# Opening of a two-block transformer kernel: who computes the scale sums, who norms the first x tiles, who makes the last two rests of h

## The chip, the core and the metric

The kernel runs on one core of a Trainium2 chip. A core has five engines that each work through their own list of instructions in order: TensorE (PE, matrix products; PEld is its weight load), VectorE (DVE), ScalarE (ACT), GpSimd (POOL) and SyncE (SP), which here issues the transfers (DMA). The engines wait for each other by semaphores. On-chip data lies in SBUF (128 partitions); matrix products are written to PSUM, in banks of 128 x 512 float32. The metric is the device time of one execution in microseconds (us); less is better.

## The reference, cut to what matters

```python
mod = (silu(c) @ w_mod).reshape(c.shape[0], 6, 1, -1)     # c: 1 x 1024, w_mod: 1024 x 6144
sa, ca, ga, sb, cb, gb = (mod[:, 0], ..., mod[:, 5])      # six rows of 1024
h = layernorm(x) * (1 + ca) + sa                          # x: 2048 tokens x 1024
x = x + ga * attention(h, wq, wk, wv, wo, beta)           # 32 heads, 4 segments of 512 tokens with a memory
h = layernorm(x) * (1 + cb) + sb
x = x + gb * token_mlp(h, w1, b1, w2, b2)                 # MLP across the 2048 tokens, width 3584
```

The change touches only how `sa` (the shift), `ca` (the scale) and the first 512 rows of `h` are computed. Each entry of `sa` and `ca` is a dot product of 1024 products, silu(c) against one column of `w_mod`.

## The kernel before, in words

Everything is float32. A product of two float32 matrices is made from three matmuls: each operand is cut into a high part `hi` (a cast, line 123 on ScalarE or 125 on another engine) and a rest `lo = x - hi` (line 126), and hi*hi, hi*lo and lo*hi are added up in PSUM. The helper is `split(dst, src, hi_eng, lo_eng)`.

The **opening** makes h for segment 0 (tokens 0 to 511) and the projections of head group 0 from it.

- Four tiles of x (128 tokens x 1024) are loaded and normed in place by `norm_x` (line 215): `ln_stats` (line 128) takes mean and variance on VectorE (lines 131 and 133) and the inverse root with ScalarE's Ln and Exp (134, 135) and a refinement on VectorE (137 to 139); then one VectorE operation of one column makes the bias (217) and ScalarE writes `x*rstd + bias` over 1024 columns (218).
- silu(c) lies in two forms: `sc`, a column per chunk, and `scb`, the whole row repeated on all 128 partitions.
- h is made in 8 chunks `ct` of 128 channels. For each chunk two pieces of `w_mod`, tiles `wm` of 128 x 1024 (512 KB), are loaded: part 0 for the shift and part 1 for the scale. The shift sums come from VectorE: one scalar_tensor_tensor multiplies `wm` by `scb` and adds up each row (line 283). The scale sums of chunks 0 to 3 (`ct < NSC`, NSC = 4) come from TensorE (line 291: eight products 128x128 by 128x1 into a PSUM column). Those of chunks 4 to 7 come from POOL and ScalarE: POOL multiplies by `scb` in two halves of 512 columns (line 287), ScalarE adds up the rows by a copy with an accumulator (line 288). Line 295 adds 1 (`saca`).
- `h_chunk` (line 220) transposes the four x tiles' 128 channels on TensorE into a PSUM bank (line 223), applies scale and shift on ScalarE (225), and splits the result: in segment 0 `hi` on ScalarE and `lo` on POOL for all eight chunks. In segment 1, `hi` is on VectorE and `lo` on VectorE for odd chunks and POOL for even.
- `first_chunk(ct)` adds the chunk's 12 matmuls into keys and values (line 196, `nps`) and 3 into queries (204, `qps`). Meanwhile the first weights are split (`wv`, `wq`: hi on ScalarE, lo on VectorE).

After the opening, segment 1 follows in the same way (`seg_load(1)`, whose x tiles 4 to 7 are loaded behind the last `wm`; `seg_chunks`, `project`): the copies of k, v and the value parts (lines 358, 359, 364, 365) and the splits of q and k into `sg` for segment 0 stand between. Then come 32 rounds of attention (4 heads each; scores, maxima, exponentials, values), the output projection, and the token MLP in two large products.

Each engine's list is ordered by a planner that simulates the program with its own costs when the kernel is built; a change in the opening thus can shift instructions of the later attention rounds against each other. The transfers of the opening have one order on SyncE's queue: x 0 to 3, then the `wm` pieces and the first weights, then x 4 to 7. Eleven `wm` buffers exist, so the twelfth piece waits for the reader of the first. The host lays out the scale part of `w_mod` per chunk in the form that its engine needs (transposed for TensorE below `NSC`, row-wise from `NSC` on).

Of the kernel before, what the change touches and what calls it, by code (L numbers as in the profile page):

```python
# [13 lines left out]
ALU = mybir.AluOpType  # L14
# [16 lines left out]
LEADP, LEADS, NSK = 8, 3, 8  # L31
XB = 4
EARLY = (2, 3)
NSC = 4
VL = 1
PHB = 2
P32B = 2
# [10 lines left out]
def attention_and_mlp(ctx, tc, x, wq, wkv, wo, beta, w1, b1, w2, b2, c, wm_a, wm_b, out):  # L48
    nc = tc.nc
    V, A, G, T, SY = nc.vector, nc.scalar, nc.gpsimd, nc.tensor, nc.sync  # L50
# [18 lines left out]
    scb, gaw = (a.tile([P, D], F32, name=n) for n in ("scb", "gaw"))  # L69
# [8 lines left out]
    def bank(tag, bufs, name):  # L78
        return psum.tile([P, 512], F32, tag=tag, bufs=bufs, name=name)
# [39 lines left out]
    def split(dst, src, hi_eng, lo_eng):  # L119

        hi, lo = dst[:, 0], dst[:, 1]
        if hi_eng is A:
            A.copy(hi, src)  # L123
        else:
            hi_eng.tensor_copy(hi, src)
        lo_eng.tensor_tensor(lo, src, hi.bitcast(F32), op=ALU.subtract)  # L126

    def ln_stats(pool, src, tag):
        st = const.tile([P, 2, 6], F32, tag="st", bufs=4, name="st")
        for i in range(2):  # L130
            V.bn_stats(st[:, i], src[:, 512 * i:512 * i + 512])
        mv = const.tile([P, 4], F32, tag="mv", bufs=4, name="mv")
        V.bn_aggr(mv[:, 0:2], st)
        A.activation(mv[:, 2:3], mv[:, 1:2], AF.Ln, bias=eps)
        A.activation(mv[:, 2:3], mv[:, 2:3], AF.Exp, scale=-0.5)
        v, r0, t = mv[:, 1:2], mv[:, 2:3], mv[:, 3:4]
        V.tensor_scalar(t, v, EPS, r0, op0=ALU.add, op1=ALU.mult)
        V.tensor_scalar(t, t, -0.5, r0, op0=ALU.mult, op1=ALU.mult)
        V.tensor_scalar(r0, t, 1.5, r0, op0=ALU.add, op1=ALU.mult)
        return mv  # L140
# [4 lines left out]
    def new_page(name):  # L145
        return page.tile([P, 2, 512], F32R, tag="page", bufs=16, name=name)
# [17 lines left out]
    def load_part(g, pr, kind, part, res):  # L164

        if pr == 0:
            split_part(g, kind, part, fetch_part(g, kind, part))
            return
        for i in range(2):
            w = aw.tile([P, 2, 512], F32R, tag="w", bufs=8, name=f"w{kind}{pr}_{g}_{part}_{i}")  # L170
            SY.dma_start(w.bitcast(F32), wsp[g, 2 * part + i if kind == "v" else 4 + i])
            res[kind, 2 * part + i] = w
# [37 lines left out]
    def load_x(pool, tt):  # L210
        t = pool.tile([P, D], F32, tag="x", bufs=XB, name=f"x{tt}")
        SY.dma_start(t, x[P * tt:P * tt + P])
        return t

    def norm_x(pool, t):
        mv = ln_stats(pool, t, "a")
        V.tensor_scalar(mv[:, 3:4], mv[:, 0:1], -1.0, mv[:, 2:3], op0=ALU.mult, op1=ALU.mult)
        A.activation(t, t, AF.Identity, scale=mv[:, 2:3], bias=mv[:, 3:4])

    def h_chunk(pool, xs, seg, ct):  # L220
        ps = bank(*(("s1", 2), ("s2", 2))[ct % 2] if seg else ("s2", 2), f"hps{seg}_{ct}")
        for i in range(4):
            T.transpose(ps[:, 128 * i:128 * i + 128], xs[i][:, P * ct:P * ct + P], ident)
        h32 = pool.tile([P, L], F32, tag="h32", bufs=HB, name=f"h32_{seg}_{ct}")
        A.activation(h32, ps, AF.Identity, scale=saca[:, ct, 1:2], bias=saca[:, ct, 0:1])
        pg = new_page(f"h{seg}_{ct}")
        split(pg, h32, V if seg else A, V if seg and ct % 2 else G)
        hpages[seg, ct] = pg

    def token_tile(tt):  # L230

        r = gaw
        norm_x(a, r)
        for half in range(2):
            ps = bank("s2", 2, f"hpl{tt}_{half}")
            for i in range(4):
                ct = 4 * half + i
                T.transpose(ps[:, 128 * i:128 * i + 128], r[:, P * ct:P * ct + P], ident)
            for i in range(4):
                ct = 4 * half + i  # L240
                A.activation(r[:, P * ct:P * ct + P], ps[:, 128 * i:128 * i + 128], AF.Identity,
                             scale=saca[:, ct, 1:2], bias=saca[:, ct, 0:1])
        hi = a.tile([P, D], F32, tag="raw", bufs=3, name=f"hix{tt}")
        A.copy(hi.bitcast(F32R), r)
        for c in (slice(0, 512), slice(512, 1024)):
            G.tensor_tensor(r[:, c].bitcast(F32R), r[:, c], hi[:, c], op=ALU.subtract)
        i = tt % 4
        for part, t in enumerate((hi, r)):
            SY.dma_start(hT1[tt // 4 - 2, :, :, part, P * i:P * i + P].rearrange("k p n -> p k n"),
                         t.rearrange("p (k n) -> p k n", k=NK))  # L250
# [4 lines left out]
    s1p = left.__enter__()  # L255
    xs = {0: [load_x(s1p, tt) for tt in range(4)]}
# [10 lines left out]
    def first_chunk(ct):  # L267
        h = hpages[0, ct]
        for half in range(2):
            kv_chunk(W[0, 0], h, half, ct, two_tiles(first[half]))  # L270
        q_chunk(W[0, 0], h, ct, first[2])

    with tc.high_priority():
        for t in xs[0]:
            norm_x(s1p, t)
    scale_ps = bank("ms", 1, "scale")
    scs = s1p.tile([P, NK], F32, name="scs")
    for ct in range(NK):
        for part in range(2):
            wm = s1p.tile([P, D], F32, tag="wm", bufs=11, name=f"wm{ct}_{part}")  # L280
            last_wm = SY.dma_start(wm, wm_a[part, ct])
            if part == 0:
                V.scalar_tensor_tensor(wm, wm, 1.0, scb, op0=ALU.mult, op1=ALU.mult, accum_out=saca[:, ct, 0:1])
            elif ct >= NSC:
                for i in range(2):
                    c = slice(512 * i, 512 * i + 512)
                    G.tensor_tensor(wm[:, c], wm[:, c], scb[:, c], op=ALU.mult)
                A.activation(wm, wm, AF.Copy, accum_out=scs[:, ct:ct + 1])
            else:
                for k in range(NK):  # L290
                    T.matmul(scale_ps[:, ct:ct + 1], wm[:, P * k:P * k + P], sc[:, k:k + 1], start=(k == 0),
                             stop=(k == NK - 1), skip_group_check=True)
        if ct < 3:
            load_part(0, 0, *(("v", 0), ("q", 0), ("v", 1))[ct], W[0, 0])
        V.tensor_scalar_add(saca[:, ct, 1:2], (scale_ps if ct < NSC else scs)[:, ct:ct + 1], 1.0)
        h_chunk(s1p, xs[0], 0, ct)
        if ct:
            first_chunk(ct - 1)
# [260 lines left out]
    def seg_load(seg):  # L559
        seg_x[seg] = [load_x(s2p, tt) for tt in range(4 * seg, 4 * seg + 4)]  # L560
        for t in seg_x[seg]:
            norm_x(s2p, t)

    def seg_chunks(seg, lo, hi):
        for ct in range(lo, hi):
            h_chunk(s2p, seg_x[seg], seg, ct)
# [63 lines left out]
    for n in range(-LEADS, 4 * NI + VL):  # L630
# [4 lines left out]
        if 0 <= m + 4 < 4 * NI:  # L635
            t = (m + 4) // 4
# [5 lines left out]
        if 59 <= m < 67:  # L642
            seg, ct = 2 + (m - 59) // 4, 2 * ((m - 59) % 4)
            reload_h(seg, ct)
            reload_h(seg, ct + 1)
        if 4 * NI - 5 <= m < 4 * NI + 3:
            i = m - 4 * NI + 5
# [282 lines left out]
    for u, (ph, g) in enumerate(units):  # L930
# [59 lines left out]
        t = tp.tile([P, 3, 512], F32, tag="tu", bufs=1, name=f"tu{g}")  # L990
# [66 lines left out]
```

## Time and profile before

| what | value |
|---|---|
| median of 3 runs | 2281.92 us (2280.88 to 2282.4) |
| the profiled execution's own time | 2281.25 us |
| its span, first to last instruction | 2279.5 us |
| granted TensorE clock, mean | 0.989 |
| TensorE busy (matmul) | 2214.7 us, 97% |
| VectorE busy | 1671.9 us, 73% |
| ScalarE busy | 1148.1 us, 50% |
| POOL busy | 735.6 us, 32% |

Times in the timeline are us from the start of the span. A timeline row gives start and duration, engine, line and operation, output and inputs, shape, and in brackets the idle time of the engine before it with what ended it; a row with x2 merges two instructions in succession. The table of windows gives how long each engine was busy in a stretch, and the granted clock as a share of full speed. The busy time of an instruction on VectorE or POOL includes time in which it has been issued but stands still.

### The profile page before, as it was taken

The page shows a single profiled execution, that of the slowest core. Times are in us where ns is not written, and L with a number is a line of the kernel's source. Part 1 is how long each engine was busy: PE and PEld are TensorE (multiplying, and loading weights), DVE is VectorE, ACT ScalarE, POOL GpSimd, SP SyncE. Part 2 cuts the span into 40 slices and gives each one's busy share as a digit, 9 for nine tenths or more (in the row PEclk, how much of TensorE's full clock was granted, in tenths as well). Part 3 has the DMA queues.
Part 4 walks back from the last instruction along what each step waited for, and adds up shares of the span by engine and source line. Part 5 has one row for each costly group of instructions (what it writes and reads, how often), then busy time and mean ns, then how long its engine had stood idle before and what let it go on. Part 6 is the DMA issues. An engine that isn't in the chain of part 4 may idle for free.

```text
span 2279.5 us, 38372 instructions
## 1 busy us (share of the span) xinstructions
PE 2214.7 (97%) x13802; PEld 1905.5 (84%) x13802; DVE 1671.9 (73%) x3798; ACT 1148.1 (50%) x2090; POOL 735.6 (32%) x843
## 2 busy tenths in 40 slices
PE   7999999999999999999999999999999999999999
PEld 6888898888988889987877887888887888888887
DVE  6676677766777677664878555788889787878787
ACT  6476677665666666654646333533334242424232
POOL 5165566655766666644000000023333000000000
PEclk9999999999999999999999999999999999999999
DMA  6656565687567566673455765556557441414134
GB/s 259 202 170 172 145 192 167 188 265 230 167 189 209 171 193 185 210 245 108 138 197 201 273 239 194 218 198 235 208 203 277 162 153 56 153 56 143 56 120 148
DMA packets 172882, 415.72 MB, mean 182 GB/s; under 512 B 17268, under 2 KB 71572, under 8 KB 163732
## 3 DMA queue, kind: packets, MB, share of 16 engines
q1 hardware_dynamic: 172692, 413.27, 55.3%
q8 instruction: 110, 1.80, 0.3%
q14 instruction: 80, 0.66, 0.1%
HBM read 237.28 MB, written 125.06 MB: 159 GB/s over the span
## 4 chain that ended last, share of the span: by engine, by line
PE 80%; DMA 7%; DVE 7%; ACT 3%; POOL 2%; issue 1%; SPq 0%; DVEq 0%; ACTq 0%; POOLq 0%
PE mx L849 39%; PE nps L196 13%; PE qps L204 8%; PE po L734 6%; PE pv L504 4%; DMA xb<-x1d 2%; DMA x1e<-xb 2%; PE a L475 1%; PE sx L440 1%; PE sz L440 1%; PE rd L412 1%; DMA sk<-nt 1%; PE a L478 1%; DVE xb L906 1%; PE up L422 1%
## 5 line engine op out<-in xcount | busy, mean ns | idle before, releaser
L849 PE MATMUL mx<-bU,sp 128*128 128x512 f32 x2352 | 535.4, 389 | 3.0 <-DVE sp L126 1.7
L849 PEld LDWEIGHTS mx<-bU,sp 128*128 128x128 f32 x2352 | 441.0, 188 | 96.9 <-DVE sp L126 2.7
L123 ACT CAST sp<-wr 128x384 fp32r<-128x384 f32 (+2 forms) x408 | 217.0, 545 | 451.7 <-PE mx L849 373.7
L196 PE MATMUL nps<-wv,h 128*128 128x256 f32 x3072 | 436.5, 283 | 3.5 <-POOL h L126 3.5
L849 PE MATMUL mx<-bA,sp 128*128 128x512 f32 x1764 | 434.4, 392 | 5.5 <-ACT sp L123 3.3
L490 POOL TENSOR_TENSOR ph<-p,ph 128x640 f16<-128x640 f32 x256 | 377.3, 1495 | 153.7 <-ACT ph L488 153.5
L196 PEld LDWEIGHTS nps<-wv,h 128*128 128x128 f32 x3072 | 404.5, 190 | 10.4 <-POOL h L126 4.7
L849 PEld LDWEIGHTS mx<-bA,sp 128*128 128x128 f32 x1764 | 332.9, 189 | 76.4 <-ACT sp L123 4.4
L126 DVE TENSOR_TENSOR sp<-wr,sp 128x384 fp32r<-128x384 f32 (+2 forms) x408 | 258.1, 643 | 32.0 <-ACT sp L123 31.9
L856 DVE TENSOR_TENSOR ac<-mx,ac 128x512 f32<-128x512 f32 x280 | 189.3, 685 | 92.8 <-PE mx L849 92.3
L204 PE MATMUL qps<-h,wq 128*128 128x512 f32 x768 | 199.9, 406 | 2.3 <-DVE pv L507 1.1
L734 PE MATMUL po<-wo,ots 128*128 128x512 f32 x768 | 183.8, 395 | 6.6 <-DVE more_x L737 2.8
L488 ACT CAST ph<-p 128x1280 f16<-128x1280 f32 x128 | 161.2, 1260 | 44.7 <-POOL p L486 44.1
L734 PEld LDWEIGHTS po<-wo,ots 128*128 128x128 f32 x768 | 144.3, 190 | 38.0 <-ACT ots L123 2.7
L441 DVE CUSTOM_DVE_ANT_0 sx<-sx,mask 128x128 f32<-128x128 f32 (+1 forms) x256 | 109.8, 429 | 86.5 <-PE sx L440 85.1
L204 PEld LDWEIGHTS qps<-h,wq 128*128 128x128 f32 x768 | 144.0, 194 | 31.3 <-issue 2.8
L849 PE MATMUL mx<-bB,sp 128*128 128x512 f32 x588 | 164.0, 389 | 0.0
L486 POOL TENSOR_SCALAR_AFFINE_SELECT p<-p 128x256 f32<-128x256 f32 x256 | 119.5, 475 | 125.3 <-ACT p L479 65.9
L504 PE MATMUL pv<-vp,ph 128*128 128x97 bf16 (+1 forms) x2560 | 144.1, 203 | 1.6 <-DVE red L511 1.3
L504 PEld LDWEIGHTS <-ph 128*128 128x128 f16 x2560 | 115.3, 99 | 25.4 <-issue 12.9
L849 PEld LDWEIGHTS mx<-bB,sp 128*128 128x128 f32 x588 | 110.5, 188 | 23.1
L856 DVE TENSOR_TENSOR cc<-mx,cc 128x512 f32<-128x512 f32 x140 | 94.2, 682 | 37.5 <-PE mx L849 37.2
(208 smaller groups left out, 3208.3 us busy)
## 6 DMA issues: line engine op xcount, KB each, us to landing
sk<-sg SPq DMA_DIRECT2D x384, 128.0 KB
wr<-in_w_dram SPq DMA_DIRECT2D x28, 1024.0 KB
wr<-in_w_dram SPq DMA_DIRECT2D x32, 768.0 KB
bstu<-ucd SPq DMA_DIRECT2D x28, 768.0 KB
wsp<-wv SPq DMA_DIRECT2D x32, 512.0 KB
rawm<-in_wm_b_dram SPq DMA_DIRECT2D x32, 512.0 KB
wv<-wsp SPq DMA_DIRECT2D x32, 512.0 KB
pcd<-cc SPq DMA_DIRECT2D x14, 1024.0 KB
```

Of the source, the lines that this page charges most:

```text
L123: A.copy(hi, src)
L126: lo_eng.tensor_tensor(lo, src, hi.bitcast(F32), op=ALU.subtract)
L196: T.matmul(ps[:, aa], h[:, j, 128 * tt:128 * tt + 128], wt[:, i, o:o + 256], start=(n == 0), stop=(n >= 6 * NK - 2), skip_group_check=True)
L204: T.matmul(ps, wt[:, i, o:o + 128], h[:, j], start=(k + n == 0), stop=(3 * k + n == 3 * NK - 1))
L441: marks[4 * t + h - LEADS, "V"] = V.tensor_tensor_reduce(o, o, mask[:, 384 - 128 * i:], 1.0, -3.0e38, op0=ALU.add, op1=ALU.max, accum_out= ...
L486: G.affine_select(w, w, pattern=[[0, 2], [1, 128]], compare_op=ALU.is_ge, fill=0.0, base=0, channel_multiplier=-1)
L488: marks[n, "A"] = A.copy(ph[:, 0], p32)
L490: marks[n, "G"] = G.tensor_tensor(ph[:, 1, c], p32[:, c], ph[:, 0, c], op=ALU.subtract)
L504: T.matmul(pv[:, i, 0:w], ph[:, part, o:o + 128], d["vp"][:, j, h, 0:w], start=(n == 0), stop=(n == 19), skip_group_check=True)
L734: T.matmul(ps, os_[:, i, P * ct:P * ct + P], wop[ct, nh][:, j], start=(n == 0), stop=(n == 3 * NK - 1))
L849: T.matmul(ps, ops[q][:, i, P * k:P * k + P], b[:, j], start=(m == 0 and first), stop=(m == 3 * nk - 1), skip_group_check=True)
L856: V.tensor_tensor(d, ps, d, op=ALU.add)
```

## The change

Three things change, all in the opening.

1. The scale sums: a string `SCALE_BY = "TGVGVGVV"` names who makes the scale sum of each chunk. Chunk 0 stays with TensorE (T). Chunks 1, 3 and 5 are POOL's with ScalarE's adding up (G). Chunks 2, 4, 6 and 7 are VectorE's (V), in the form of the shift sums: one scalar_tensor_tensor with an accumulator. So chunks 1 and 3 go from TensorE to POOL and ScalarE, chunk 2 from TensorE to VectorE, chunks 4, 6 and 7 from POOL and ScalarE to VectorE; chunk 5 stays. `NSC` is now 1, which also changes the host's layout of the scale part for chunks 1 to 3.
2. Of the first four x tiles, 1 and 3 are normed by one VectorE tensor_scalar, (x - mean) * rstd, over 1024 columns, in the place of the bias operation and ScalarE's pass.
3. The rests `lo` of h for chunks 6 and 7 of segment 0 are made by VectorE in the place of POOL.

```diff
-NSC = 4
+NSC = 1
+SCALE_BY = "TGVGVGVV"
...
-    def norm_x(pool, t):
+    def norm_x(pool, t, on_v=False):
         mv = ln_stats(pool, t, "a")
+        if on_v:
+            V.tensor_scalar(t, t, mv[:, 0:1], mv[:, 2:3], op0=ALU.subtract, op1=ALU.mult)
+            return
         V.tensor_scalar(mv[:, 3:4], mv[:, 0:1], -1.0, mv[:, 2:3], op0=ALU.mult, op1=ALU.mult)
         A.activation(t, t, AF.Identity, scale=mv[:, 2:3], bias=mv[:, 3:4])
...
-        split(pg, h32, V if seg else A, V if seg and ct % 2 else G)
+        split(pg, h32, V if seg else A, V if (ct % 2 if seg else ct > 5) else G)
...
-        for t in xs[0]:
-            norm_x(s1p, t)
+        for i, t in enumerate(xs[0]):
+            norm_x(s1p, t, i % 2)
...
             if part == 0:
                 V.scalar_tensor_tensor(wm, wm, 1.0, scb, op0=ALU.mult, op1=ALU.mult, accum_out=saca[:, ct, 0:1])
-            elif ct >= NSC:
+            elif SCALE_BY[ct] == "V":
+                V.scalar_tensor_tensor(wm, wm, 1.0, scb, op0=ALU.mult, op1=ALU.mult, accum_out=scs[:, ct:ct + 1])
+            elif SCALE_BY[ct] == "G":
                 for i in range(2):
                     c = slice(512 * i, 512 * i + 512)
                     G.tensor_tensor(wm[:, c], wm[:, c], scb[:, c], op=ALU.mult)
```

## The prediction

> **What bounds the kernel now.** I read the page first, then the chain of waits from 0 to 140 us, then the timelines of VectorE, POOL and ScalarE beside each other, and the table of windows for the clock.
>
> ```profile
> span 2279.5 us, 38372 instructions
> PE 2214.7 (97%) x13802; PEld 1905.5 (84%) x13802; DVE 1671.9 (73%) x3798; ACT 1148.1 (50%) x2090; POOL 735.6 (32%) x843
> ```
>
> TensorE is busy 97% of the span; 65 us are all that it stands. A good part of that is in the first 60 us, which the change edits. What TensorE does not wait for there cannot pay; what it waits for longer is added, unless a later gap takes it up. The chain of waits shows whom it waits for:
>
> ```profile
> 31.70 5.00 POOL wm L287 x4
> ...
> 37.20 1.73 POOL h L126
> ...
> 43.63 2.49 POOL wm L287 x2
> 46.12 1.24 POOL h L126
> 47.40 1.21 PE nps L196 x8
> ...
> 53.32 0.34 ACT k L358
> ```
>
> From 31.7 to 47.4 us POOL carries the chain, with scale sums (L287) and rests of h (L126). At 47.3 the rest of chunk 5 is done; the last three chunks' matmuls then end the opening at 53.3, 6.0 us later. So far POOL looks like the thing to unload, and the change unloads it. But the two timelines say what POOL's time is made of. VectorE first, then POOL:
>
> ```profile
> 15.55 1.22 DVE L283 SCALAR_TENSOR_TENSOR wm<-wm,scb 128x1024 f32<-128x1024 f32 x1
> 17.47 1.29 DVE L126 TENSOR_TENSOR wv<-rawv,wv 128x512 fp32r<-128x512 f32 x2 [0.63 <-ACT wv L123]
> 25.35 2.28 DVE L283 SCALAR_TENSOR_TENSOR wm<-wm,scb 128x1024 f32<-128x1024 f32 x1
> 35.57 2.22 DVE L283 SCALAR_TENSOR_TENSOR wm<-wm,scb 128x1024 f32<-128x1024 f32 x1
> 38.29 1.73 DVE L283 SCALAR_TENSOR_TENSOR wm<-wm,scb 128x1024 f32<-128x1024 f32 x1
> 46.00 1.23 DVE L131 BATCH_NORM_STATS2 st<-x 128x6 f32<-128x512 f32 x2
> 58.87 0.42 DVE L125 CAST h<-h 128x512 fp32r<-128x512 f32 x1
> 59.53 1.41 DVE L125 CAST h<-h 128x512 fp32r<-128x512 f32 x1 [0.24 <-ACT h L225]
> ```
>
> ```profile
> 23.61 2.95 POOL L126 TENSOR_TENSOR h<-h,h 128x512 fp32r<-128x512 f32 x2 [14.46 <-ACT h L123]
> 31.70 5.00 POOL L287 TENSOR_TENSOR wm<-wm,scb 128x512 f32<-128x512 f32 x4
> 38.90 3.50 POOL L287 TENSOR_TENSOR wm<-wm,scb 128x512 f32<-128x512 f32 x2
> 49.60 1.28 POOL L126 TENSOR_TENSOR h<-h,h 128x512 fp32r<-128x512 f32 x1 [1.00 <-DVE mv L133]
> 59.37 1.28 POOL L126 TENSOR_TENSOR h<-h,h 128x512 fp32r<-128x512 f32 x1 [4.20 <-DVE h L125]
> ```
>
> Alone, a VectorE sum takes 1.22 us and a POOL half 5.00/4 = 1.25. But the sum issued at 35.57 took 2.22: POOL's four ran until 36.70, and from there 1.1 us were left for it. The sum at 25.35 took 2.28: POOL's second rest ended at 26.56. The other way round, POOL's two halves at 38.90 took 3.50, not 2.5: the sum of 38.29 ran until 40.02. A VectorE cast of 0.42 took 1.41 beside POOL's rest of 59.37. The statistics at 46.00, with one input, took their usual 0.61 each beside POOL's rest of 46.12. So a POOL product and a VectorE product or cast from SBUF exclude each other whole, in the order in which they come. Moving such work from POOL to VectorE does not put it beside POOL's; it stands in the same queue of two engines. That is the bound that I use.
>
> The Trainium skill, SBUF — State Buffer, section "Who interferes with whom", says this as a rule: a VectorE instruction with two SBUF inputs, or in a two-port mode, excludes a POOL instruction that reads SBUF, and one with a single input outside these modes does not. The trace agrees (2.22 against 1.22 us; statistics unmoved). It speaks against this change.
>
> **The change part by part.** I have the issue order of the changed program, built but not run. Between 14.4 us (the first shift sum is done, alike in both) and the end of the last rest, I count the work that excludes.
> - Before: VectorE 7 shift sums x 1.22 + 6 rests of weights x 0.65 (1.29/2) = 12.4; POOL 8 halves and 8 rests x 1.25 = 20.0. Together 32.4 us. The last rest ends at 49.60 + 1.28 = 50.9, so of 36.5 us the pair stood idle for 4.1.
> - The scale sums of chunks 1 and 3 (TensorE to POOL): 4 halves, +5.0. Chunk 2 (TensorE to VectorE): +1.2. Chunks 4, 6, 7 (POOL to VectorE): 3 x (1.22 - 2.5) = -3.8. Sum +2.4.
> - Rests of chunks 6 and 7: 2 x (0.65 - 1.25) = -1.2.
> - Norms of x 1 and 3 on VectorE: no row has a tensor_scalar of 128x1024. Nearest are the cast (0.42 for 512, so 0.84, excluding) and the sum (1.22). I take 0.8, the cast's, as it too reads one tensor, and keep 1.2 as the other end: two are +1.6 (to 2.4).
>
> Together 32.4 + 2.4 - 1.2 + 1.6 = 35.2 us, 2.8 more, against 4.1 idle that could take it up. On ScalarE two norms of 1.2 go, and one of four adding-up copies. What TensorE loses is this:
>
> ```profile
> 12.49 3.57 PE L291 MATMUL scale<-sc,wm 128*128 128x1 f32 x16 [3.42 <-DMA wm<-in_wm_a_dram]
> 37.02 1.04 PE L223 MATMUL hps<-ident,x 128*128 128x128 f32 x8
> 69.21 5.92 PE L196 MATMUL nps<-wv,h 128*128 128x256 f32 x48 [0.51 <-POOL h L126]
> ```
>
> Three such groups, about 3.6 us each before 35 us, while TensorE waits anyway: worth nothing, since its work after 47.4 (6.0 us) is the same in both.
>
> Does the order fill the idle time? I walked both issue orders with these durations: an instruction starts when its engine, its inputs and (for the excluding kinds) the other engine's product allow. In the order of before the last three rests' start and the end come out at 48.3 and 54.0 (trace: 47.3 and 53.3), so the walk runs 0.7 long. In the changed order the steps are:
> - Norm of x 1 from 15.0, POOL's chunk-1 halves 16.3 to 19.6 around the norm of x 3, weight rests, a shift sum: scale 0 is added at 22.1, not at 16.5, because it is queued on VectorE behind the norms, two weight rests and a sum that alternate with POOL.
> - h chunk 0 and its rest: 25.9 (before 24.7). Sums of chunk 2 and POOL's halves of chunk 3 alternate until 30.8.
> - h chunks 1 and 2 wait for scale 1, which stands on VectorE behind the sum of chunk 2: 29.7. Their rests end at 33.3 and 35.8, between the sums of chunks 3 and 4.
> - VectorE has both sums of chunk 4 and two shift sums to do before POOL's next rest: rests 3 and 4 end at 42.0 and 44.5.
> - POOL's halves of chunk 5 stand in its list behind rests 3 and 4, and last from 45.7 to 48.2. ScalarE adds up and makes h:
>
> ```profile
> 34.25 1.06 ACT L288 ACTIVATE wm<-wm 128x1024 f32<-128x1024 f32 x1 [4.41 <-POOL wm L287]
> 35.22 0.18 ACT L288 ACTIVATION_READ_ACCUMULATOR wm<-wm 128x1 f32 x1
> 35.69 0.78 ACT L225 ACTIVATE h<-hps,saca 128x512 f32<-128x512 f32 x1 [0.29 <-DVE saca L295]
> 51.05 2.36 ACT L218 ACTIVATE x<-x,mv 128x1024 f32<-128x1024 f32 x2
> 53.31 0.35 ACT L358 COPY k<-nps 128x256 f32<-128x256 f32 x1
> 54.88 1.27 ACT L218 ACTIVATE x<-x,mv 128x1024 f32<-128x1024 f32 x1
> 56.02 0.61 ACT L123 CAST sg<-qps 128x512 fp32r<-128x512 f32 x1
> 58.01 1.49 ACT L225 ACTIVATE h<-hps,saca 128x512 f32<-128x512 f32 x2
> ```
>
> - 48.2 + 1.2 (L288) + 0.1 + 0.7 (L225) and the casts: rest 5 ends at 52.9, where the same walk had 48.3 before. Rests 6 and 7 follow on VectorE by 55.4; three chunks of matmuls end at 58.6 against 54.0. **Opening: +4.6 us.** Ends: -1.3 if all the idle 4.1 is used (35.2 against 36.5), +6 with norms of 1.2 and one more sum lost to an alternation.
>
> **Segment 1** is moved too, and this is not in the diff. Its x tiles are normed from statistics on VectorE. Before, VectorE makes these from 40 us on, in POOL's shadow, and ScalarE norms three tiles before the copy at 53.31; one follows at 54.88 and h starts at 58.01, 4.7 after the opening's end. In the changed order the statistics stand behind the last scale sum (50.8), so all four norms fall behind the copies: six copies (53.31 to 54.88, 1.6), four norms (2.36 for two, 4.7), five passes for q, k and v (four from 56.02 to 58.01, so 2.5) are 8.8, begun 1.0 before TensorE's last chunk ends. h of segment 1 starts 7.8 behind the opening's end: **+3.1 us**. Of this some returns: from the first h to the last key matmul of this segment (69.21 + 5.92 = 75.1) before took 17.1 us, while TensorE's own need is 96 x 0.123 + 20 x 0.13 = 14.4; ScalarE now has fewer passes between. Between 0 and -2.7; I take **-1.2**.
>
> ```profile
> 58.00:60.00 2.00, 1.18 (x6) 1.11 (x6) 1.76 (x4) 2.00 (x5) 0.63 (x1) 0.57 0.46 96
> 60.00:62.00 2.00, 2.00 (x13) 2.00 (x12) 1.97 (x3) 1.68 (x4) 0.66 (x1) 0.58 0.88 186
> 124.00:126.00 2.00, 0.88 (x7) 0.53 (x7) 2.00 (x10) 0.62 (x3) 2.00 (x3) 1.00 0.47 101
> 134.00:136.00 2.00, 1.86 (x7) 1.76 (x8) 2.00 (x11) 0.77 (x3) 2.00 (x4) 0.50 0.76 220
> 138.00:140.00 2.00, 2.00 (x6) 1.52 (x6) 0.69 (x1) 2.00 (x4) 0.76 (x3) 0.50 1.02 287
> ```
>
> In these windows the columns behind the length are busy TensorE, its loads, VectorE, ScalarE, POOL, then the granted clock, the DMA share and GB/s. After the gap at 53 to 58 us the clock is at 0.57 for 4 us, which costs 1.7; after a gap of about 8 us I count the same 1.7 (0 to +2 on top). The transfers keep their order; the reader of the buffer that chunk 7's shift piece reuses is now ScalarE's copy at 25.6 instead of TensorE, 1 to 2 us later, and that piece is not read before 44: nothing. Nor does the later order give a sum: it differs in many single places in the attention rounds (the first maxima are issued earlier among the matmuls of segment 1), which I can only bound by the gaps there: +-4 us, 0 taken.
>
> **Sum:** 4.6 + 3.1 - 1.2 = +6.5 us on the profiled execution's own 2281.25, which is 0.7 below the median of the runs: 2287.8 us. What can be told from no change is about 0.2%, 4.6 us: below 2277.3 is faster, above 2286.5 slower.
>
> **Rivals.**
> - *The clock stays down* (slower). With TensorE's wait of 8 us in place of 5, and sparse work as at 134 to 140 (0.50 for 6 us), another stretch at half clock costs 3 to 5: 2292. For it: both dips follow thin work. Against: the dip at 58 was short.
> - *The later rounds take it up* (no change). The place is 120 to 140 us: 2.2 us of waits and 6 us at half clock, worth 3. If the new order closes it, 6.5 - 5 = +1.5: 2283. For it: that gap is VectorE's. Against: there VectorE is busy 2.00 of 2.00 us, and nothing is taken from it.
> - *The exclusion does not bind* (faster). If VectorE's sums slipped between POOL's, the same walk without exclusion ends the opening at 47.1, 6.9 below: 2274. It decides if the sums of chunks 2 and 4 run beside POOL in 1.2 us. Against: 2.22, 2.28 and 3.50 above. A weaker form: only the idle 4.1 is used and the new order of the rounds gives 4 more: 2277.
>
> The Trainium skill, VectorE: DVE Perf Modes, section "Mode 2×_2P — use both read ports for one tensor", lets a float32 tensor_scalar in SBUF run at double speed with both ports. The cast's 0.42 for 512 columns agrees; by it the norm is about 0.6 (estimate), the sum 0.4 less, and it excludes POOL.
>
> **How the numbers follow.** The forecast has 0.50, the clock 0.15, both slower; the later rounds 0.18 and small forms of the forecast near the bound make up "same"; faster forms 0.15. The range must reach into both: 2276 to 2295. The forecast's own is 2284 to 2292. Faster 0.15, same 0.2, slower 0.65.
>
> **What would show it.** VectorE's sums of chunks 2 to 7 at 1.7 to 2.5 us; POOL's halves of chunk 5 late, around 45; first copy of k at about 57; all four norms of segment 1 behind it, its first h at 65; a longer gap of TensorE before 66. I am wrong if the copy of k comes before 54, or if the sums stay at 1.2 beside POOL.

## The result, and the profile after

The change made the kernel slower: 2306.62 us median of 4 runs (2302.42 to 2307.24) against 2281.4 us of the kernel before (4 runs, 2279.94 to 2282.4). The ratio is 1.0105 with an interval of 1.009 to 1.012, so between 20.5 and 27.4 us of 2281 were lost; 6.5 were predicted. The profiled execution took 2307.24 us, 26.0 more than that of before. The page's header of the changed kernel:

```profile
span 2305.5 us, 38265 instructions
PE 2220.3 (96%) x13754; PEld 1906.0 (83%) x13754; DVE 1678.0 (73%) x3808; ACT 1141.1 (49%) x2086; POOL 736.5 (32%) x839
```

TensorE has 48 matmuls fewer (13754 against 13802) and yet is busy 5.6 us longer. The three groups of scale products that went lasted 3.41, 3.58 and 1.84 us in the kernel before (at 17.47, 22.20 and 33.17 us), 8.8 together; so the other matmuls take 14.4 us longer (5.6 + 8.8), and the remaining 11.6 of the 26.0 are waits. The matmuls are longer where the clock is low; its mean fell from 0.989 to 0.984, which by itself is some 11.8 us at full speed (0.016 x 2305.5 - 0.011 x 2279.5, from rounded means).

The chain of waits of the changed kernel, start and length in us:

```profile
39.82 2.26 POOL h L127
42.08 3.46 POOL wm L293 x2
...
45.56 1.16 ACT wm L294 x2
```

POOL still carries the chain of the opening: a rest of h that stood behind a sum of VectorE, then the scale sum of chunk 5, then ScalarE's adding up. The first copy of k comes at 56.95; before it was at 53.31. The timelines of VectorE and POOL show why:

```profile
14.26 0.81 DVE L219 TENSOR_SCALAR x<-x,mv 128x1024 f32<-128x1024 f32 x1
...
26.09 2.29 DVE L289 SCALAR_TENSOR_TENSOR wm<-wm,scb 128x1024 f32<-128x1024 f32 x1
...
38.64 2.30 DVE L289 SCALAR_TENSOR_TENSOR wm<-wm,scb 128x1024 f32<-128x1024 f32 x1
...
46.81 1.22 DVE L289 SCALAR_TENSOR_TENSOR wm<-wm,scb 128x1024 f32<-128x1024 f32 x1
```

```profile
30.59 4.57 POOL L127 TENSOR_TENSOR h<-h,h 128x512 fp32r<-128x512 f32 x2 [1.08 <-ACT h L124]
...
42.04 3.49 POOL L293 TENSOR_TENSOR wm<-wm,scb 128x512 f32<-128x512 f32 x2
49.02 1.27 POOL L127 TENSOR_TENSOR h<-h,h 128x512 fp32r<-128x512 f32 x1 [3.49 <-ACT h L124]
```

The new scale sums (L289) of chunks 2 and 6 in their places beside POOL take 2.29 and 2.30 us; the last, with POOL idle, 1.22. POOL's two rests at 30.59 take 4.57 instead of 2.5. The norm takes 0.81. ScalarE, from the end of the opening on:

```profile
56.95 0.37 ACT L364 COPY k<-nps 128x256 f32<-128x256 f32 x1 [2.25 <-PE nps L197]
...
63.88 2.40 ACT L222 ACTIVATE x<-x,mv 128x1024 f32<-128x1024 f32 x2
68.33 2.12 ACT L229 ACTIVATE h<-hps,saca 128x512 f32<-128x512 f32 x3 [2.05 <-PE hps L227]
...
80.55 0.37 ACT L364 COPY k<-nps 128x256 f32<-128x256 f32 x1 [3.52 <-PE nps L197]
```

The four norms (L222) of segment 1 end at 66.28, and then ScalarE waits 2.05 us for TensorE, which has the memory update in front of the transposes, at half clock:

```profile
66.12 1.97 PE L428 MATMUL up<-v,pk 128*128 128x132 f32 x8
67.88 1.06 PE L227 MATMUL hps<-ident,x 128*128 128x128 f32 x4
```

h of segment 1 starts at 68.33 (before 58.01), and the first copy of its keys, at 80.55, is 9.4 us later than in the kernel before:

```profile
71.16 0.37 ACT L358 COPY k<-nps 128x256 f32<-128x256 f32 x1 [3.97 <-PE nps L196]
```

The clock by windows (after the length: busy TensorE, weight loads, VectorE, ScalarE, POOL; then the granted clock, the DMA share and GB/s), of the changed kernel and then of the kernel before:

```profile
47.00:54.00 7.00, 6.12 (x24) 5.31 (x25) 6.89 (x14) 4.26 (x8) 3.96 (x7) 0.51 0.01 2
60.80:71.00 10.20, 7.16 (x30) 6.06 (x31) 5.83 (x15) 7.62 (x12) 1.40 (x2) 0.50 0.60 127
```

```profile
47.00:54.00 7.00, 6.60 (x48) 6.22 (x49) 4.17 (x21) 6.65 (x16) 5.94 (x10) 1.00 0.01 4
60.80:71.00 10.20, 9.69 (x80) 9.47 (x79) 8.63 (x13) 3.69 (x5) 4.08 (x4) 0.96 0.97 277
```

Two stretches of some 7 and 10 us that ran at full speed now run at half: the same 7 us hold 24 matmuls instead of 48.

Compared copy by copy, the delay is 9.4 us at the first keys of segment 1, 13 to 15 at 113 to 137 us, between 7 and 19 until about 390 us (the places change order, so the delay goes up and down), and 26.1 at ScalarE's last copy of a round's result, `ot`, at the end of attention (1108.1 against 1082.0 us, shown below). So more than half of the loss, 16.7 us, is made in the attention rounds, which the diff doesn't touch.

### The profile page after: what moved, and what is told of

It reads as the page before. It is cut to its first block, busy times and chain, and to the rows that moved or that the text cites. A ratio compares the mean times of both kernels' runs of the same rounds, so it can differ in the third digit from the quotient of the medians.

```text
span 2305.5 us, 38265 instructions
## 1 busy us (share of the span) xinstructions
PE 2220.3 (96%) x13754; PEld 1906.0 (83%) x13754; DVE 1678.0 (73%) x3808; ACT 1141.1 (49%) x2086; POOL 736.5 (32%) x839
## 4 chain that ended last, share of the span: by engine, by line
PE 78%; DMA 9%; DVE 6%; ACT 2%; POOL 2%; issue 1%; SPq 1%; DVEq 0%; ACTq 0%; POOLq 0%
PE mx L855 39%; PE nps L197 12%; PE qps L205 8%; PE po L740 7%; PE pv L510 3%; DMA xb<-x1d 2%; DMA x1e<-xb 2%; POOL ph L496 1%; DMA sk<-nt 1%; PE a L481 1%; PE sx L446 1%; PE sz L446 1%; DMA wm<-in_wm_a_dram 1%; PE rd L418 1%; PE a L484 1%
## 5 line engine op out<-in xcount | busy, mean ns | idle before, releaser
L197 PE MATMUL nps<-wv,h 128*128 128x256 f32 x3072 | 442.2, 286 | 2.1 <-ACT h L124 1.0
L197 PEld LDWEIGHTS nps<-wv,h 128*128 128x128 f32 x3072 | 410.1, 193 | 10.4 <-POOL h L127 2.4
L510 PEld LDWEIGHTS <-ph 128*128 128x128 f16 x2560 | 116.0, 99 | 28.9 <-issue 12.4
L482 ACT ACTIVATE p<-a,shift 128x512 f32<-128x512 f32 x128 | 88.2, 689 | 80.9 <-PE a L481 63.2
```

The costliest lines, as they stand in the source:

```text
L197: T.matmul(ps[:, aa], h[:, j, 128 * tt:128 * tt + 128], wt[:, i, o:o + 256], start=(n == 0), stop=(n >= 6 * NK - 2), skip_group_check=True)
L510: T.matmul(pv[:, i, 0:w], ph[:, part, o:o + 128], d["vp"][:, j, h, 0:w], start=(n == 0), stop=(n == 19), skip_group_check=True)
```

## The experiments

The theories: the loss is the opening's, carried through to the end; or it comes from the later instructions, which the build put into another order; or each has a share. And for the opening: it is the exclusion of VectorE and POOL that costs, or the longer lists alone. Each ratio below is against the kernel before on the same chip, with its 95% interval; "us of 2281" is that ratio times 2281.

### The opening and the later order, each alone

The order behind the opening was pinned. For each engine, the instructions behind the opening are chained in a given order by edges that only bind the issue order and add no wait; `LATER` holds that order, taken from the other build. In the traces the order of the opening's own instructions stayed as it was. The kernel before pinned to its own order was not run by itself; so pinned, with only its shift sums read from PSUM, it comes out at 0.9988 (below), so the edges cost little.

```diff
+LATER = (
...
+def in_order(tc, first):
+    """Keep each engine's instructions traced from `first` on in the order LATER."""
...
+                if last is not None:
+                    tc.add_manual_dep(i, last.name, info, reason="later order")
+                last = i
...
     left.__exit__(None, None, None)
+    behind_opening = len(nc.cur_bb.bb.instructions)
...
+    in_order(tc, behind_opening)
```

**The changed opening with the later order of before:**

> The changed kernel, but everything traced behind the opening keeps, engine by engine, the issue order that it has in the kernel before. In the changed kernel the keys of segment 1 come 8 us late at 76 us, 13 us late at about 100 us, and the copies to the output of the attention rounds are 26 us late at their end. Theory A (the opening loses some 8 to 13 us, and the rest is lost to another issue order of the attention rounds): 2290 to 2295 us, and the delay at the end of attention is that at 100 us. Theory B (a late opening puts the engines out of step, and the rounds lose the rest whatever their order): 2303 to 2307 us.

Measured: 2292.09 us, ratio 1.0057 (1.004 to 1.0075), 13.0 us of 2281 (9.1 to 17.1): the time of theory A.

**The opening of before with the later order of the changed kernel:**

> The kernel before with its own opening, but everything traced behind the opening keeps the issue order that it has in the changed kernel. Theory A: the issue order alone costs about 12 us, 2291 to 2296 us, with the opening's first copy of k at 53 us as before. Theory B: the order costs nothing, 2280 to 2283 us.

Measured: 2293.07 us, ratio 1.0067 (1.0044 to 1.0089), 15.3 us (10.0 to 20.3), theory A again.

The two together, 28.3, stand against 24.0 for both (20.5 to 27.4); within the intervals they add up. So neither theory of one cause holds: by the times, about half is the opening and about half the order of work that nobody edited.

The traces, one execution of each kernel, give the opening less. The copies `ot` at the end of attention, in the kernel before, the changed kernel, the changed opening with the old order and the old opening with the new order (shortest, middle and longest copy in ns, then the first and the last start in us):

```profile
L521 ACT COPY ot<-ops x32: 565/586/618, 136.0 to 1082.0; 128x512 f32<-128x512 f32 x32
L527 ACT COPY ot<-ops x32: 561/587/643, 148.7 to 1108.1; 128x512 f32<-128x512 f32 x32
L671 ACT COPY ot<-ops x32: 566/586/618, 141.6 to 1088.0; 128x512 f32<-128x512 f32 x32
L667 ACT COPY ot<-ops x32: 558/587/644, 143.1 to 1093.4; 128x512 f32<-128x512 f32 x32
```

The opening alone is 6.0 us late there, as theory A had it (6.2 at the first keys); its other 4.5 us of that execution (10.5 in all) arise behind the attention, in work that both kernels issue in the same order, and were not taken apart. The order alone is 11.4 late, the changed kernel 26.1. So 17.4 of these 26.1 are the parts taken alone; whether the rest is the two acting together or a difference between executions stays open.

ScalarE's rows show one thing that the order decides, first for the changed opening with the old order, then for the old opening with the new order:

```profile
57.28 2.36 ACT L365 ACTIVATE x<-x,mv 128x1024 f32<-128x1024 f32 x2
59.55 0.35 ACT L508 COPY k<-nps 128x256 f32<-128x256 f32 x1
```

```profile
52.28 0.37 ACT L504 COPY k<-nps 128x256 f32<-128x256 f32 x1 [3.38 <-PE nps L341]
```

In the old order three norms of segment 1 stand in front of the first copy and delay it to 59.55 (6.2 us later than before), but then segment 1 loses no more: its first keys are copied at 77.39 against 71.16, again 6.2. In the new order the copy comes first, 1.0 earlier than before, and the norms behind it cost segment 1 about 4.5 (75.68 against 71.16).

### Does the exclusion carry the opening's loss?

The second operand of VectorE's sums, silu(c), is put into two PSUM banks that are free in the opening, and each sum is made in two halves of 512 columns; later order as before.

```diff
+    for i in range(2):
+        ps = bank(("pv", "s1")[i], (1, 2)[i], f"scpv{i}")
+        for j in range(4):
+            T.transpose(ps[:, 128 * j:128 * j + 128], bc[:, 4 * i + j], ident)
+        scp.append(ps)
...
+    def row_sum(wm, ct, part, dst):
+        for i in range(2):
+            c = slice(512 * i, 512 * i + 512)
+            V.scalar_tensor_tensor(wm[:, c], wm[:, c], 1.0, scp[i], op0=ALU.mult, op1=ALU.mult,
+                                   accum_out=acc2[:, ct, part, i:i + 1])
+        V.tensor_tensor(dst, acc2[:, ct, part, 0:1], acc2[:, ct, part, 1:2], op=ALU.add)
...
-                V.scalar_tensor_tensor(wm, wm, 1.0, scb, op0=ALU.mult, op1=ALU.mult, accum_out=saca[:, ct, 0:1])
+                row_sum(wm, ct, part, saca[:, ct, 0:1])
```

**In the changed kernel:**

> The changed kernel with the old order behind the opening, in which VectorE's sums over w_mod read silu(c) from two PSUM banks instead of SBUF, in two halves of 512 columns each, so that each of them reads a single tensor from SBUF. If VectorE and POOL exclude each other because both read two tensors from SBUF: a whole sum takes 1.3 to 1.5 us also while POOL is at work (2.2 to 2.3 us in the changed kernel), the first copy of k comes before 52 us (57 us in the changed kernel), and the time falls by 5 to 8 us against the run with the old order. If VectorE simply has too much work there: halves of 1.1 us beside POOL, the copy at 56 to 58 us, and no change of the time.

Measured: 2280.83 us (10 runs), ratio 1.0005 (0.9991 to 1.0019): 1.1 us, against 13.0 with the sums read from SBUF. 11.9 us of the opening's 13.0 are gone, more than the 5 to 8 expected. Besides the operand's place, each sum now has two halves and an addition, and POOL's first half of chunk 5 moved ahead of a rest in its list. VectorE and POOL of this kernel:

```profile
23.61 1.70 DVE L270 TENSOR_TENSOR wq<-rawq,wq 128x512 fp32r<-128x512 f32 x1
...
36.21 0.16 DVE L424 TENSOR_TENSOR saca<-acc 128x1 f32<-128x1 f32 x1
36.29 0.68 DVE L422 SCALAR_TENSOR_TENSOR wm<-wm,scpv 128x512 f32<-128x512 f32 x1
...
37.62 1.21 DVE L424 TENSOR_TENSOR scs<-acc 128x1 f32<-128x1 f32 x1
```

```profile
36.27 1.30 POOL L451 TENSOR_TENSOR wm<-wm,scb 128x512 f32<-128x512 f32 x1
37.53 1.28 POOL L270 TENSOR_TENSOR h<-h,h 128x512 fp32r<-128x512 f32 x1
```

The half sum at 36.29 runs in 0.68 us beside POOL's product of 36.27, which takes its usual 1.30. But what still reads two operands from SBUF still waits: the weight rest at 23.61, and even an addition of one column, 1.21 us at 37.62 behind POOL's rest of 37.53, where the one at 36.21 took 0.16. So for these instructions with two operands the exclusion goes by where the operands lie, not by the size or the engine's load. The first copy of k is at 54.22, 5.3 earlier than with the sums in SBUF, but not before 52 as expected: in the old order the norms still stand in front of it. These 5.3 us are what the trace shows of the 11.9; where the other 6.6 come from is not shown.

**In the kernel before** (shift sums only):

> The kernel before, with the old order behind the opening, its shift sums on VectorE reading silu(c) from PSUM in two halves. Exclusion by two SBUF inputs: POOL's products lose the 1.0, 0.5 and 0.5 us that they stand still between 35 and 42 us, and the sums of 2.2 us become 1.4; the copy of k comes 1 to 4 us earlier than 53.3 us, 2277 to 2281 us. Otherwise no change, 2281 to 2283 us.

Measured: 2276.36 us (10 runs), ratio 0.9988 (0.9975 to 1.0), 0.6 below the range expected. POOL's two halves, which took 3.50 beside a shift sum, and the copy that ends the opening (53.31 before):

```profile
37.29 2.54 POOL L445 TENSOR_TENSOR wm<-wm,scb 128x512 f32<-128x512 f32 x2
```

```profile
50.79 0.34 ACT L517 COPY k<-nps 128x256 f32<-128x256 f32 x1
```

The opening is 2.5 us shorter, within the 1 to 4 expected. The time is 2.7 us shorter (0 to 5.7); as the interval touches 0, a gain in time is likely but not shown.

The Trainium skill, SBUF — State Buffer, section "Who interferes with whom", says that a VectorE instruction contends with POOL's reads when both of its inputs lie in SBUF, and not with at most one there, outside the two-port modes. These runs agree: 0.68 us for a half beside POOL with one input in PSUM, so 1.36 for a sum, against 2.29 for the whole sum with both in SBUF.

### The three parts, one at a time

Each part alone on the kernel before, later order as before; the edits are shown against the changed kernel, and put the other parts back. The scale sums alone:

```diff
-            norm_x(s1p, t, i % 2)
+            norm_x(s1p, t)
...
-        split(pg, h32, V if seg else A, V if (ct % 2 if seg else ct > 5) else G)
+        split(pg, h32, V if seg else A, V if seg and ct % 2 else G)
```

> Only the scale sums changed (TGVGVGVV), norms and rests as before, everything behind the opening in the old order. All three parts in this order cost 11 us, with the first copy of k 6 us late. Counted by work that excludes, the sums add 2.4 us, the norms 1.6, and the rests take 1.2 away. If the sums carry the loss, as they alternate with POOL on the path of every chunk: copy of k 3 to 7 us late, 2286 to 2293 us. If they do not: within 2 us of before.

Measured: 2286.91 us, ratio 1.0032 (1.002 to 1.0045), 7.3 us, in the range for sums that carry the loss; first copy of k 2.8 us later than before, a little under the 3 to 7 expected:

```profile
56.10 0.35 ACT L508 COPY k<-nps 128x256 f32<-128x256 f32 x1
```

The two norms alone (`NSC = 4`, `SCALE_BY = "TTTTGGGG"`, rests as before):

> Only x tiles 1 and 3 normed by VectorE, the rest as before, old order behind the opening. POOL has no product before 23.6 us here, so the two norms of 0.8 us exclude nothing: copy of k within 1 us of 53.3, time within 3 us of before (2278 to 2284 us). If VectorE's queue is what counts: copy 1.5 to 3 us late, 2283 to 2286 us.

Measured: 2284.25 us, ratio 1.0012 (1.0003 to 1.0021), 2.7 us; copy 2.4 later, where at most 1 was expected unless VectorE's list counts. It counts. The third shift sum and the copy, first the sum in the kernel before:

```profile
20.85 1.22 DVE L283 SCALAR_TENSOR_TENSOR wm<-wm,scb 128x1024 f32<-128x1024 f32 x1
```

```profile
21.94 2.29 DVE L430 SCALAR_TENSOR_TENSOR wm<-wm,scb 128x1024 f32<-128x1024 f32 x1
...
55.70 0.35 ACT L508 COPY k<-nps 128x256 f32<-128x256 f32 x1
```

```profile
21.82 1.34 POOL L270 TENSOR_TENSOR h<-h,h 128x512 fp32r<-128x512 f32 x1 [12.48 <-ACT h L267]
```

Two norms of 0.81 push the third shift sum, alone before (1.22 us), to 21.94, where POOL's first rest of h now already runs: 2.29. A small delay on one engine turned into an encounter with the other.

The rests of chunks 6 and 7 alone (`NSC = 4`, `SCALE_BY = "TTTTGGGG"`, norms as before):

> Only the rests of chunks 6 and 7 made by VectorE, the rest as before, old order behind the opening. POOL's last rest but two ends at 47.3, TensorE then works 6 us without a wait, so an earlier rest 6 or 7 gives nothing: copy of k within 1 us of 53.3 and time within 3 us of before (2278 to 2284 us).

Measured: 2282.88 us, ratio 1.0018 (1.0008 to 1.0027), 4.1 us; copy 0.8 later, both as expected:

```profile
54.11 0.37 ACT L508 COPY k<-nps 128x256 f32<-128x256 f32 x1 [0.56 <-PE nps L340]
```

The copies add up: 2.8 + 2.4 + 0.8 = 6.0, against 6.2 with all three. The times, 7.3 + 2.7 + 4.1 = 14.1, stand against 13.0. The sums are half of it. No part gains, not even the one that takes work off POOL. Why the rests lose 4.1 us with a copy only 0.8 late is not shown.

### Where the later order costs

The kernel before, whose order up to the attention rounds is kept, with only the rounds in the order of the changed kernel (the first added line now stands where the rounds begin):

```diff
     right = tc.tile_pool(name="late2", bufs=1, side="right", reuse_waits="tile")
+    behind_opening = len(nc.cur_bb.bb.instructions)
...
+    in_order(tc, behind_opening)
```

> The kernel before with its own opening and its own order in segment 1; only what is traced from the attention rounds on keeps the issue order of the changed kernel. With segment 1 in the new order too it took 12 us more than before, of which 5 were there at the keys of segment 1. If the rounds' order costs the rest by itself: 2286 to 2290 us, nothing lost at 76 us. If the rounds only suffer from a late segment 1: 2280 to 2283 us.

Measured: 2291.39 us, ratio 1.0048 (1.0033 to 1.0064), 10.9 us, somewhat above the 2290 expected. Nothing is lost until the keys of segment 1 (74.66 against 75.17 for their second copy); at 89 us it is 5.3 behind and at 123 us 7.9. So the rounds' order costs 10.9 us by itself. Together with the 4.5 that the new order costs in segment 1 that is 15.4, close to the 15.3 measured for the new order as a whole. The traces don't bear this sum out: the last `ot` is 12.4 us late with the rounds' order alone and 11.4 with segment 1 in the new order too, so the 4.5 are not seen again there.

Then the same, split at step 32 of the 128 steps of the rounds: the first 32 in the new order and the rest in the old, and the other way round.

```diff
+    in_order(tc, at_rounds, at_mid, EARLY_ROUNDS)
+    in_order(tc, at_mid, None, LATE_ROUNDS)
```

> The kernel before with its own opening and segment 1; of the attention rounds, what is traced in the first 32 of 128 steps keeps the changed kernel's issue order, the later steps the old one. The whole of the rounds in the new order costs 11 us; its copies to the output are 8 us late at 361 us, near the end of these steps. If the loss is an early one (maxima products that stand one behind the other while TensorE waits for VectorE, from 79 us on): 2286 to 2290 us. If it comes from the many small places later: 2280 to 2284 us.

> The reverse: the first 32 steps in the old order, the later ones in the changed kernel's order. If the loss is an early one: 2281 to 2285 us. If it comes from the many small places later: 2287 to 2292 us.

Measured: early 2291.2 us, ratio 1.004 (1.0025 to 1.0054), 9.1 us; late 2285.22 us, ratio 1.0016 (1.0004 to 1.0029), 3.6 us; together 12.7, against 10.9 for the rounds as a whole. Most of it is in the first 32 steps, as the theory of an early loss has it (both times lie just above its ranges). The windows 81 to 87 and 86 to 91 us of the kernel with early rounds new, then with late rounds new:

```profile
81.00:87.00 6.00, 3.51 (x18) 2.72 (x17) 4.65 (x13) 3.53 (x7) 0.00 (x0) 0.95 0.83 240
86.00:91.00 5.00, 5.00 (x32) 5.00 (x31) 3.33 (x10) 1.29 (x3) 0.00 (x0) 0.66 0.87 190
```

```profile
81.00:87.00 6.00, 6.00 (x48) 5.75 (x47) 3.96 (x12) 3.52 (x7) 0.00 (x0) 1.00 1.02 397
86.00:91.00 5.00, 5.00 (x45) 4.95 (x44) 3.84 (x13) 0.37 (x1) 0.00 (x0) 1.00 0.97 240
```

TensorE is busy 3.51 of 6 us instead of 6.00, and then runs at 0.66 of its clock. What stands there, with early rounds new, TensorE and VectorE:

```profile
83.16 0.38 PE L591 MATMUL sy<-sk 96*128 96x256 f32 x1 [0.79 <-DVE mx L592]
...
85.56 0.50 PE L591 MATMUL sz<-sk 96*128 96x512 f32 x1 [1.71 <-DVE mx L592]
86.58 4.17 PE L347 MATMUL nps<-wv,h 128*128 128x256 f32 x21
```

```profile
83.22 1.29 DVE L277 TENSOR_TENSOR wv<-rawv,wv 128x512 fp32r<-128x512 f32 x2
84.42 0.68 DVE L277 TENSOR_TENSOR sg<-qps,sg 128x512 fp32r<-128x512 f32 x1
```

and in the kernel before:

```profile
82.34 0.34 PE L440 MATMUL sy<-sk 96*128 96x256 f32 x1
82.51 3.35 PE L196 MATMUL nps<-wv,h 128*128 128x256 f32 x28
```

The new order puts the short score products of a round one behind the other; each needs the bank of an earlier one, whose maximum (`mx`) stands on VectorE behind rests of weights and of q. The old order has 28 projection matmuls between them, which start without a wait here. TensorE loses the 2.5 us that it waits (6.00 - 3.51) and another 1.7 in the half clock of 3.4 us that follows (21 matmuls in 4.17 us against 28 in 3.35): 4.2 of the 5.4 that are lost at 89 us. The places of the loss beyond 100 us (from 5.4 at 89 us to 7.9 at 360, 9.5 at 510 and 12.0 at the last `ot`, in an execution that ended 13.2 behind) were not taken apart, nor those of the late steps; that stays open.

### A version that is faster than both

With VectorE's second operand in PSUM, scale sums can be moved to it after all. These two kernels are the kernel before with the shift sums in that form, and with scale sums of chunks 4 to 7 moved as the string says. Two of them, norms and rests as before, later order as before:

```diff
 NSC = 4
+SCALE_BY = "TTTTGVGV"
```

> The opening of before with silu(c) for VectorE in PSUM, and the scale sums of chunks 5 and 7 moved from POOL and ScalarE to VectorE in that form; norms and rests as before; old order behind the opening. If only the two-tensor reads from SBUF made the move costly, POOL loses 5 us of products on its path from 30 to 47 us and nothing comes back: first copy of k at 46 to 49 us (53.3 in before, 50.8 with the shift sums alone in this form), 2270 to 2276 us. If another wait takes its place (VectorE's queue, ScalarE): copy at 50 to 53 us, 2276 to 2281 us.

Measured: 2279.59 us (12 runs), ratio 1.0 (0.999 to 1.0009). The copy of k is at 52.26, 1.0 earlier, so the second case of the expectation came: another wait took the place of the old one. TensorE's last product of the opening and ScalarE's norms of segment 1 show which:

```profile
48.74 0.85 PE L348 MATMUL qps<-h,wq 128*128 128x512 f32 x3
```

```profile
49.99 2.36 ACT L365 ACTIVATE x<-x,mv 128x1024 f32<-128x1024 f32 x2
52.26 0.35 ACT L523 COPY k<-nps 128x256 f32<-128x256 f32 x1
```

TensorE has done its part of the opening at 49.6, and the copy stands behind the norms. Why nothing of the 1.0 is left at the end stays open.

All four of POOL's:

```diff
 NSC = 4
+SCALE_BY = "TTTTVVVV"
```

> As the run before it, with the scale sums of all of chunks 4 to 7 on VectorE in this form, so that POOL makes nothing but the rests of h in the opening. POOL's path is then 10 us shorter, but the last piece of w_mod lands at about 35.5 us and TensorE has 17 us of products and 4 of transposes from 24 us on, which bounds the end of the opening at about 46 us: copy of k at 46 to 50 us, 2269 to 2276 us, little better than with two chunks moved. If VectorE's queue becomes the wait: copy at 50 us or later, 2275 to 2281 us.

Measured: 2275.8 us (12 runs), ratio 0.9981 (0.9969 to 0.9994): 4.3 us faster than the kernel before (1.4 to 7.1), and the fastest kernel here, though its gain over the old sums read from PSUM (0.9988) is within the intervals.

```profile
47.76 2.36 ACT L365 ACTIVATE x<-x,mv 128x1024 f32<-128x1024 f32 x2
50.02 0.35 ACT L523 COPY k<-nps 128x256 f32<-128x256 f32 x1
```

The opening ends 3.3 us earlier, and the copy is again held by ScalarE's norms of segment 1 in front of it. Copy and time lie where the two cases of the expectation meet.

## Why the prediction was right about the sign and wrong about the size

The forecast summed the opening and segment 1, and put the clock and the new order of the attention rounds at nothing. The step that failed is the last of these: the new order alone costs 10.9 us. Segment 1 and the clock were too small besides. Term by term:

- **The bound (right).** "A POOL product and a VectorE product or cast from SBUF exclude each other whole": sums of 2.29 and 2.30 us beside POOL, 1.22 alone, and the first copy of k came 5.3 us earlier, the time fell by 11.9, when one operand was moved to PSUM. The rival "the exclusion does not bind" falls.
- **The norms (right in price).** 0.8 was taken, 0.81 measured. That their place in VectorE's list delays other work was in the walk; alone they cost 2.4 us at the first copy.
- **TensorE's removed groups (right in effect).** "About 3.6 us each" was misread: the third took 1.84. Nothing hung on it. TensorE's later work came no earlier for them; at none of the places compared above is it ahead.
- **Opening, +4.6 (a little too large: +3.6).** The first copy of k was forecast at about 57 and came at 56.95, in part by luck, since two errors went against each other. The rest of chunk 5 ends at 50.3 (49.02 + 1.27), not at 52.9; the walk made more of the alternation than there was, and POOL's halves of chunk 5 began at 42.04 instead of 45.7. But the last three chunks took 6.7 us (50.3 to 56.95) instead of 6.0, since they began at half clock until 54 us, which the sum had not charged.
- **Segment 1, +3.1 - 1.2 = +1.9 (mis-sized: +5.8).** The step was right: all four norms fell behind the copies. The ScalarE passes were counted at 8.8 us and lasted 9.3 (56.95 to 66.28). What was missing is TensorE: the memory update stood in front of the last transposes and held h for another 2.05 us, and the whole stretch from 60.8 to 71 us ran at half clock. h came 11.4 us after the first copy (before 4.7), so +6.7, of which 0.9 returned by the first keys, not 1.2.
- **"0 to +2" for the clock (too small).** The rival "the clock stays down" was right in its mechanism (more half clock behind longer waits and thin work), and its place is earlier and longer than it said: 7 us at 0.51 within the opening and 10 us at 0.50 in segment 1. Its time, 2292, was too low all the same, because it left out the next point.
- **"It differs in many single places in the attention rounds ... +-4 us, 0 taken" (the step that failed).** The new order of the rounds alone costs 10.9 us, and with segment 1 15.3; in the changed kernel's trace 16.7 us are lost between the first keys of segment 1 and the end of attention. The bound of 4 came from the gaps that the trace of before shows there; a new order makes new gaps. In the issue lists it was visible that the first maxima moved earlier among the matmuls, and this was told and then priced at nothing. With 3.6 + 5.8 measured and a term of 10.9 the sum is 20.3, against 24.0 for the ratio of the two kernels; the upper end of the interval of the 10.9 (7.5 to 14.6) just holds the difference. The 3.6 and 5.8 are from one execution of each kernel, and hold the clock's loss there.
- **The rival "the later rounds take it up" falls for the changed kernel.** There the rounds lose 16.7 us. With the old order it has some truth, at the place that it named: the changed opening is 6.3 us behind at 123 us, 4.3 at 160 and 2.5 from 550 to 780 us. But at the end of attention it is 6.0 behind again.

The Trainium skill, TensorE: Matmul & The Clock Gate, section "What's actually happening", says that the clock falls to half after an idle window of about 3.4 us, the windows running freely. The traces agree in the length: behind the first 31 us, the half-clock stretches are 3.4, 6.8 or 10.2 us long. They also show it after thin work: with the early rounds new, TensorE's longest wait between 81 and 87 us is 1.71 us, and it was busy 3.51 of these 6 us; half clock follows from 86.5.

## What to carry to other kernels

Before work is moved from POOL to VectorE to balance them, count POOL's products and VectorE's two-operand work and casts from SBUF as one queue; moving one of VectorE's operands to PSUM took its sums out of that queue here. Where a planner orders a kernel, an edit of 50 us can reorder the other 2200: compare the issue orders, price what stands directly in front of what TensorE waits for, and measure edit and order apart by pinning the order. A wait of TensorE can cost twice, as here at 81 to 91 us: 2.5 us as the wait and 1.7 in the clock that follows.

## What was not expected of the hardware

- An addition of one column, two operands of 128x1 in SBUF, waits for POOL like a large product: 1.21 us at 37.62 against 0.16 alone.
- The order of instructions that was changed by no one is worth 0.5 to 0.7% of the time (1.0048 for the rounds, 1.0067 with segment 1), as much as the edit itself (1.0057).
- The runs of the kernel before spread over 2272 to 2284 us on one chip, so a difference of 3 to 4 us could only be told from 10 to 12 runs.
